# Spilling converted weights through GpSimd's DMA queue in place of SyncE's

## The chip, the core and the metric

The kernel runs on one core of a Trainium2 chip. The metric is the device time of one execution in microseconds (us). The core's engines work side by side, each through its own instructions in a fixed order: TensorE (PE; matmuls into PSUM), VectorE (DVE), ScalarE (ACT), GpSimd (POOL) and SyncE (SP). An engine waits at an instruction until what it needs is there, and everything behind it on that engine waits too. SyncE, GpSimd and ScalarE can ask for DMA transfers between the chip's large memory (DRAM) and its working memory (SBUF); each has its own queue of requests, and the transfers themselves run on 16 shared DMA engines.

## The reference

```python
def reference(q, k, v, cap, w1, w2, w3, w4, g):          # names shortened
    s = cap * tanh((q @ k.T) / sqrt(64) / cap)           # 4 batches, 12 heads, 448 x 448
    x = softmax(s) @ v                                   # -> 1792 tokens x 768
    h = x @ w1                                           # 768 -> 2048
    y = (h - tanh(h)) @ w2                               # 2048 -> 768
    h = y @ w3                                           # 768 -> 1024
    e = h * softmax(h)
    return ((e - mean(e)) / sqrt(var(e) + 1e-6) * g) @ w4   # 1024 -> 768
```

The weights come as 64-bit floats. The result is needed in 32 bits.

## The kernel before

**Halves and stages.** The four batches are done in two halves of two batches (`hb` 0 and 1), 896 tokens each. Each half runs through `attention`, `moe1` (w1, the tanh term and w2) and `moe2` (w3, softmax, norm and w4). Matmuls are done as three products of high and low parts (fp32r), so a weight is kept as a tile `w` of [128, 2, 512], high part first.

**Conversion and spill.** In the first half each weight unit is loaded as raw 64-bit words into a tile `st` (three buffers; line 106). VectorE puts a 32-bit float together in a tile `f` with three instructions (lines 111, 112, 113), ScalarE writes the high part into `w` (line 119, or 125 for w4), and VectorE the low part (line 120, or 126). There are 72 units. Each converted tile of 512 KB is then written to DRAM once by `keep` (line 136, "spill"): in order, five units behind the conversion (`DD` is 5), and the rest at the end of a stage. In the second half a unit is only read back from there (line 191, or 153 during attention). The tiles `w` take turns in 13 buffers, with one more (`wx`) in `moe1`; a buffer is free again when TensorE has used it and its spill has landed.

**Units of the first stage.** During attention the first 13 units are loaded by GpSimd's queue (in one case SyncE's) and converted beside it. Their spills stand at the end of that stage, in the `while pending: keep()` loop.

**moe1.** `up` (lines 459, 461) computes a block of 36 matmuls into a PSUM tile `hp`; `nonlinear` then has ScalarE (lines 487, 489, 491, 495, 501) and VectorE (493, 497, 496, 498, 502) turn it into `gh` and `gl`. Line 496, `t = h - t`, is the last to read `hp`. After the first four, the blocks share two PSUM buffers, so a block can begin when line 496 of the block two before it is done. `down` (lines 515, 517) multiplies by w2, and VectorE adds the result to `acc` (line 524). The weights for what follows are converted between these instructions.

**moe2.** `norm` ends in one GpSimd instruction, `rstd` to the power -0.5 (line 560); VectorE computes its input (line 559) and uses its output (line 561) ahead of TensorE's transposes (line 564).

**Order.** Attention is written out in order. In the other stages a scheduler orders the instructions of each engine ahead of time by its own estimate of durations and of what waits for what. So a change on one queue can move instructions on all engines.

```python
            pending.append((key, w))
            if len(pending) > DD:
                keep()
```

Of the kernel before, what the change touches and what calls it, by code (L numbers as in the profile page):

```python
# [9 lines left out]
F32 = mybir.dt.float32  # L10
# [19 lines left out]
def fused_kernel(ctx, tc, qk_in, v, cap, w1, w2, w3, w4, gln, out):  # L30
    nc = tc.nc
# [101 lines left out]
    def keep():  # L133
        key, w = pending.pop(0)
        d = drw.tile([P, 2, 512], F32R, name=f"d{key}")
        nc.sync.dma_start(d.bitcast(F32), w.bitcast(F32))
        saved[key] = d

    ahead = {}
# [38 lines left out]
    def unit(key, src, n, scale=None):  # L178

        pool, n2 = place["pool"]  # L180
        i = place["at"] = (place["at"] + 1) % (WA + n2)
        if key in ahead:
            w = ahead.pop(key)
            return w[:, 0], w[:, 1]
        if i < WA:
            w = wp.tile([P, 2, 512], F32R, tag="w", name="w")
        else:
            w = pool.tile([P, 2, 512], F32R, tag="wx", name="wx", bufs=n2)
        hi, lo = w[:, 0], w[:, 1]
        if key in saved:  # L190
            nc.sync.dma_start(w.bitcast(F32), saved[key].bitcast(F32))
        else:
            convert(hi, lo, src, n, scale)
# [3 lines that stand above are left out]
        return hi, lo  # L197
# [31 lines left out]
    def attention(ap, hb, xh, xl, rest=None):  # L229
# [214 lines left out]
        while pending:  # L444
            keep()
# [90 lines left out]
    def moe2(mp, hb, yh, yl):  # L536
# [113 lines left out]
        while pending:  # L650
            keep()
# [105 lines left out]
```

## Time and profile before

| what | us |
|---|---|
| median of 3 runs | 907.37 |
| lowest and highest run | 906.84, 908.77 |
| the profiled execution, its own time | 907.26 |
| its span in the trace | 905.5 |
| TensorE busy | 897.6 |
| VectorE busy | 613.4 |
| ScalarE busy | 416.7 |
| GpSimd busy | 48.1 |

The span runs from the first to the last instruction; the 1.76 us beside it are start and end of the execution. Busy is the time in which an engine has an instruction of its own in work; asking for transfers doesn't count. All times in the trace are us from the span's start. The first half of the work ends around 450 us. Matmuls overlap, so TensorE shows as busy even where it could go a little faster.

### The profile page before, as it was taken

The page shows a single profiled execution, that of the slowest core. Times are in us where ns is not written, and L with a number is a line of the kernel's source. Part 1 is how long each engine was busy: PE and PEld are TensorE (multiplying, and loading weights), DVE is VectorE, ACT ScalarE, POOL GpSimd, SP SyncE. Part 2 cuts the span into 40 slices and gives each one's busy share as a digit, 9 for nine tenths or more (in the row PEclk, how much of TensorE's full clock was granted, in tenths as well). Part 3 has the DMA queues.
Part 4 walks back from the last instruction along what each step waited for, and adds up shares of the span by engine and source line. Part 5 has one row for each costly group of instructions (what it writes and reads, how often), then busy time and mean ns, then how long its engine had stood idle before and what let it go on. Part 6 is the DMA issues. An engine that isn't in the chain of part 4 may idle for free.

```text
span 905.5 us, 12979 instructions
## 1 busy us (share of the span) xinstructions
PE 897.6 (99%) x5162; PEld 727.9 (80%) x5162; DVE 613.4 (68%) x954; ACT 416.7 (46%) x469; POOL 48.1 (5%) x88
## 2 busy tenths in 40 slices
PE   8999999999999999999999999999999999999998
PEld 5444699999989998888865448999999999888887
DVE  6687989899999990988257985970543634306841
ACT  7999276446254231443279871852512502113311
POOL 2211000000000000001022200000000000000000
PEclk9999999999999999999999999999999999999999
DMA  8554680796875873730256623433242432231301
GB/s 292 183 181 149 229 324 24 237 343 210 268 267 177 320 244 126 255 134 36 102 184 198 209 92 116 134 107 113 73 140 71 138 99 87 70 131 33 128 35 53
DMA packets 46424, 142.98 MB, mean 158 GB/s; under 512 B 10460, under 2 KB 13532, under 8 KB 46364
## 3 DMA queue, kind: packets, MB, share of 16 engines
q1 hardware_dynamic: 39180, 112.95, 36.6%
q0 software_dynamic: 7040, 29.20, 9.4%
q8 instruction: 41, 0.67, 0.3%
q14 instruction: 19, 0.16, 0.1%
q10 hardware_dynamic: 144, 0.00, 0.0%
HBM read 98.64 MB, written 43.33 MB: 157 GB/s over the span
## 4 chain that ended last, share of the span: by engine, by line
PE 84%; DVE 10%; DMA 3%; issue 1%; ACT 1%; SPq 0%; DVEq 0%
PE op L515 14%; PE hp L459 14%; PE op L517 7%; PE hp L461 7%; PE o L307 7%; PE hp L226 4%; PE hp L227 4%; PE hp L225 4%; PE s L275 4%; PE oab L615 2%; PE oab L619 2%; PE oab L616 2%; PE so L324 2%; DMA st<-in_moe_w_out_dram 2%; PE x L281 2%; PE tp L564 1%
## 5 line engine op out<-in xcount | busy, mean ns | idle before, releaser
L459 PE MATMUL hp<-xh,w 128*128 128x448 f32 x384 | 115.8, 368 | 1.5 <-DVE t L496 1.5
L459 PE MATMUL hp<-xl,w 128*128 128x448 f32 x384 | 115.8, 367 | 0.0
L461 PE MATMUL hp<-xh,w 128*128 128x448 f32 x384 | 115.7, 367 | 0.0
L517 PE MATMUL op<-gh,w 128*128 128x448 f32 x336 | 96.4, 367 | 0.0
L515 PE MATMUL op<-gl,w 128*128 128x448 f32 x336 | 96.1, 367 | 0.0
L515 PE MATMUL op<-gh,w 128*128 128x448 f32 x336 | 96.1, 367 | 0.0
L459 PEld LDWEIGHTS hp<-xh,w 128*128 128x128 f32 x384 | 71.8, 188 | 10.5 <-issue 2.5
L461 PEld LDWEIGHTS hp<-xh,w 128*128 128x128 f32 x384 | 72.1, 188 | 7.4 <-issue 0.7
L459 PEld LDWEIGHTS hp<-xl,w 128*128 128x128 f32 x384 | 72.1, 188 | 7.4 <-issue 0.7
L307 PE MATMUL o<-t,vf 128*32 128x448 f32 x768 | 77.8, 542 | 0.0
L299 ACT ACTIVATE t<-t,shift,capt 128x3136 f32<-128x3136 f32 (+2 forms) x26 | 72.8, 2807 | 0.7
L524 DVE TENSOR_TENSOR acc<-op,acc 128x448 f32<-128x448 f32 x72 | 41.9, 619 | 45.7 <-PE op L517 45.7
L515 PEld LDWEIGHTS op<-gl,w 128*128 128x128 f32 x336 | 63.1, 188 | 5.9
L515 PEld LDWEIGHTS op<-gh,w 128*128 128x128 f32 x336 | 63.0, 188 | 5.9
L517 PEld LDWEIGHTS op<-gh,w 128*128 128x128 f32 x336 | 63.1, 188 | 5.8
L292 ACT ACTIVATE t<-s,tscale 128x1344 f32<-128x1344 f32 x48 | 63.5, 1379 | 5.7 <-PE s L275 5.7
L225 PE MATMUL hp<-w,xh 128*128 128x512 f32 x168 | 65.5, 390 | 0.0
L227 PE MATMUL hp<-w,xl 128*128 128x512 f32 x168 | 65.4, 389 | 0.0
L226 PE MATMUL hp<-w,xh 128*128 128x512 f32 x168 | 65.4, 389 | 0.0
L501 ACT CAST gh<-gf 128x896 fp32r<-128x896 f32 x32 | 30.1, 944 | 73.8 <-PE op L517 47.8
L493 DVE SCALAR_TENSOR_TENSOR gf<-u,hp 128x896 f32<-128x896 f32 x32 | 34.8, 1088 | 41.2 <-ACT t L489 41.2
L487 ACT ACTIVATE u<-hp 128x896 f32<-128x896 f32 x32 | 29.5, 922 | 68.3 <-PE hp L461 68.3
(161 smaller groups left out, 1670.6 us busy)
## 6 DMA issues: line engine op xcount, KB each, us to landing
d<-w SPq DMA_DIRECT2D x69, 512.0 KB
w<-d SPq DMA_DIRECT2D x56, 512.0 KB
st<-in_moe_w_out_dram SPq DMA_DIRECT2D x35, 512.0 KB
st<-in_moe_w_in_dram SPq DMA_DIRECT2D x25, 512.0 KB
kq<-in_qk_dram POOLq DMA_DIRECT2D x21, 480.0 KB, 4.0
w<-d POOLq DMA_DIRECT2D x13, 512.0 KB, 5.2
st<-in_moe_w_in_dram POOLq DMA_DIRECT2D x11, 512.0 KB, 5.1
vf<-in_v_dram POOLq DMA_DIRECT2D x22, 256.0 KB, 3.2
```

Of the source, the lines that this page charges most:

```text
L225: nc.tensor.matmul(ps, sh, mh, start=first, stop=False)
L226: nc.tensor.matmul(ps, sh, ml, start=False, stop=False)
L227: nc.tensor.matmul(ps, sl_, mh, start=False, stop=last)
L275: nc.tensor.matmul(s[b // 3][:, b % 3, :S], st[rows, cs], mv[rows, KW:], start=first, stop=last)
L292: nc.scalar.activation(t[:, 3 * half:3 * half + 3], s[half][:, :, :S], AF.Tanh, scale=tscale)
L299: nc.scalar.activation(t[:, sl], t[:, sl], AF.Exp, bias=shift, scale=capt)
L307: nc.tensor.matmul(o[cs, :S], vf[:, r, cs], t[:, 6 if r == 3 else 2 * r + g // 2], start=(r == 0), stop=(r == 3))
L459: nc.tensor.matmul(hp[:, g, :S], wh[:, ms], xs[g][i], start=(kk == 0 and i == 0), stop=False)
L461: nc.tensor.matmul(hp[:, g, :S], wl[:, ms], xs[g][0], start=False, stop=(kk == NK - 1))
L515: nc.tensor.matmul(op[:, g, :S], wh, gg[i][:, g], start=(m == 0 and i == 0), stop=False)
L517: nc.tensor.matmul(op[:, g, :S], wl, gg[0][:, g], start=False, stop=(m == nm - 1))
L524: nc.vector.tensor_tensor(a, op[:, g, :S], a, ALU.add)
```

## The change

`keep` asks for the spill through GpSimd's queue and no longer through SyncE's. The data, the sizes and the number of transfers stay the same.

```diff
     def keep():
         key, w = pending.pop(0)
         d = drw.tile([P, 2, 512], F32R, name=f"d{key}")
-        nc.sync.dma_start(d.bitcast(F32), w.bitcast(F32))
+        nc.gpsimd.dma_start(d.bitcast(F32), w.bitcast(F32))
         saved[key] = d
```

The order of instructions changes on all engines of the first half. Three places follow.

VectorE, end of attention and the first block of `moe1`: `f<-st` are the three conversion instructions, line 493 the first instruction on a finished block. Before:

```order
L112 SCALAR_TENSOR_TENSOR f<-st,f 128x512
L113 SCALAR_TENSOR_TENSOR f<-st,f 128x512
L493 SCALAR_TENSOR_TENSOR gf<-u,hp 128x896
L497 SCALAR_TENSOR_TENSOR gf<-w,gf 128x896
L496 TENSOR_TENSOR t<-hp,t 128x896
```

And now:

```order
L112 SCALAR_TENSOR_TENSOR f<-st,f 128x512
L113 SCALAR_TENSOR_TENSOR f<-st,f 128x512
L111 TENSOR_SCALAR f<-st 128x512
L112 SCALAR_TENSOR_TENSOR f<-st,f 128x512
L493 SCALAR_TENSOR_TENSOR gf<-u,hp 128x896
L113 SCALAR_TENSOR_TENSOR f<-st,f 128x512
L497 SCALAR_TENSOR_TENSOR gf<-w,gf 128x896
L496 TENSOR_TENSOR t<-hp,t 128x896
```

One more unit is converted here, two of its instructions ahead of line 493 and one behind it.

VectorE in the third group of `up` blocks, between the ninth and the tenth line 496 of the program (`w<-f,w` is the low part of a converted unit). Before:

```order
L496 TENSOR_TENSOR t<-hp,t 128x896
L120 TENSOR_TENSOR w<-f,w 128x512
L498 COPY_PREDICATED gf<-mk,t 128x896
L111 TENSOR_SCALAR f<-st 128x512 x2
L112 SCALAR_TENSOR_TENSOR f<-st,f 128x512
L502 TENSOR_TENSOR gl<-gf,gh 128x896
L113 SCALAR_TENSOR_TENSOR f<-st,f 128x512
L493 SCALAR_TENSOR_TENSOR gf<-u,hp 128x896
L112 SCALAR_TENSOR_TENSOR f<-st,f 128x512
L496 TENSOR_TENSOR t<-hp,t 128x896
```

And now:

```order
L496 TENSOR_TENSOR t<-hp,t 128x896
L497 SCALAR_TENSOR_TENSOR gf<-w,gf 128x896
L120 TENSOR_TENSOR w<-f,w 128x512
L498 COPY_PREDICATED gf<-mk,t 128x896
L120 TENSOR_TENSOR w<-f,w 128x512
L111 TENSOR_SCALAR f<-st 128x512 x2
L112 SCALAR_TENSOR_TENSOR f<-st,f 128x512
L502 TENSOR_TENSOR gl<-gf,gh 128x896
L493 SCALAR_TENSOR_TENSOR gf<-u,hp 128x896
L113 SCALAR_TENSOR_TENSOR f<-st,f 128x512
L496 TENSOR_TENSOR t<-hp,t 128x896
```

Line 497 now stands behind the first of the two, a second line 120 has come in, and one line 112 has moved ahead.

GpSimd around the norms of the first half (the `d` tiles are spills, `kq` and `vf` loads for the second half's attention). Before, its row of seven `rstd` follows the loads:

```order
L243 DMA kq<-in_qk_dram 128x960 x3
L249 DMA vf<-in_v_dram 128x512
L560 TENSOR_TENSOR rstd<-rstd,mhalf 128x1 x7
L243 DMA kq<-in_qk_dram 128x960
```

And now:

```order
L136 DMA d_3_3790<-w 128x1024
L136 DMA d_4_3803<-w 128x1024
L560 TENSOR_TENSOR rstd<-rstd,mhalf 128x1 x2
L136 DMA d_5_3805<-w 128x1024
L136 DMA d_5_3807<-w 128x1024
L136 DMA d_6_3809<-w 128x1024
L136 DMA d_7_3811<-w 128x1024
L136 DMA d_7_3813<-w 128x1024
L560 TENSOR_TENSOR rstd<-rstd,mhalf 128x1 x5
```

All 72 spills stand in GpSimd's order now: 13 behind its last load of the first attention, 48 ahead of the four loads that stood ahead of `rstd`, six between those loads and the first `rstd`, and the last five between the second and the third.

## Rows read from the trace of the kernel before

**Rows 1.** Page, part 1: busy us (share of the span) xinstructions.

```profile
PE 897.6 (99%) x5162; PEld 727.9 (80%) x5162; DVE 613.4 (68%) x954; ACT 416.7 (46%) x469; POOL 48.1 (5%) x88
```

**Rows 2.** Windows: stretch, its us, busy us by engine, PEclk, DMA share, GB/s.

```profile
170.00:190.00 20.00, 20.00 (x99) 18.16 (x98) 17.11 (x29) 9.60 (x17) 0.00 (x0) 1.00 0.97 312
...
250.00:275.00 25.00, 23.46 (x115) 21.15 (x114) 23.28 (x35) 14.45 (x19) 0.00 (x0) 1.00 0.73 252
275.00:335.00 60.00, 60.00 (x298) 55.62 (x297) 58.91 (x101) 20.07 (x31) 0.00 (x0) 1.00 0.72 252
```

**Rows 3.** Timeline of TensorE at four block starts: start, us, [idle before <-releaser].

```profile
202.96 0.37 PE L459 MATMUL hp<-xh,w 128*128 128x448 f32 x1
...
210.26 0.57 PE L459 MATMUL hp<-xh,w 128*128 128x448 f32 x2
...
262.76 0.44 PE L459 MATMUL hp<-xh,w 128*128 128x448 f32 x1 [1.25 <-DVE t L496]
...
270.58 0.44 PE L459 MATMUL hp<-xh,w 128*128 128x448 f32 x1 [0.29 <-DVE t L496]
```

**Rows 4.** Timeline of VectorE, first L493 and the four gates.

```profile
122.24 1.09 DVE L493 SCALAR_TENSOR_TENSOR gf<-u,hp 128x896 f32<-128x896 f32 x1 [2.12 <-ACT t L489]
...
201.63 1.08 DVE L496 TENSOR_TENSOR t<-hp,t 128x896 f32<-128x896 f32 x1
...
208.85 1.09 DVE L496 TENSOR_TENSOR t<-hp,t 128x896 f32<-128x896 f32 x1
...
260.53 1.08 DVE L497 SCALAR_TENSOR_TENSOR gf<-w,gf 128x896 f32<-128x896 f32 x1
261.53 1.08 DVE L496 TENSOR_TENSOR t<-hp,t 128x896 f32<-128x896 f32 x1
...
269.35 1.08 DVE L496 TENSOR_TENSOR t<-hp,t 128x896 f32<-128x896 f32 x1
```

**Rows 5.** Waits of SyncE's queue: us in total, times, longest.

```profile
SPq L106 <- DVE f L113: 89.8, 42, 7.6
```

**Rows 6.** Timeline of SyncE's queue: spills after attention, one later load.

```profile
105.17 14.82 SPq L136 DMA_DIRECT2D d<-w  x13
...
179.06 0.33 SPq L106 DMA_DIRECT2D st<-in_moe_w_out_dram  x1
```

**Rows 7.** Timeline of VectorE in a run of conversions.

```profile
178.35 0.68 DVE L113 SCALAR_TENSOR_TENSOR f<-st,f 128x512 uint32<-128x512 uint32 x1
...
181.24 0.43 DVE L111 TENSOR_SCALAR f<-st 128x512 uint32<-128x512 uint32 x1 [1.61 <-DMA st<-in_moe_w_out_dram]
181.58 0.69 DVE L113 SCALAR_TENSOR_TENSOR f<-st,f 128x512 uint32<-128x512 uint32 x1
182.18 0.69 DVE L120 TENSOR_TENSOR w<-f,w 128x512 fp32r<-128x512 f32 x1
182.79 0.69 DVE L112 SCALAR_TENSOR_TENSOR f<-st,f 128x512 uint32<-128x512 uint32 x1
...
184.85 0.43 DVE L111 TENSOR_SCALAR f<-st 128x512 uint32<-128x512 uint32 x1 [0.18 <-DMA st<-in_moe_w_out_dram]
```

**Rows 8.** Waits of VectorE for loads, 119 to 275.

```profile
DVE f L111 <- DMA st<-in_moe_w_out_dram: 4.4, 4, 1.6
...
DVE f L111 <- DMA st<-in_moe_w_in_dram: 1.0, 1, 1.0
```

**Rows 9.** Timeline of GpSimd: last load of attention, third rstd.

```profile
79.88 0.54 POOL L106 DMA_DIRECT2D st<-in_moe_w_out_dram  x1 [2.00 <-DVE rs L361]
...
407.37 0.55 POOL L560 TENSOR_TENSOR rstd<-rstd,mhalf 128x1 f32<-128x1 f32 x1 [18.81 <-DVE rstd L559]
```

**Rows 10.** Page, part 6: issues by GpSimd, KB each, median us to landing.

```profile
w<-d POOLq DMA_DIRECT2D x13, 512.0 KB, 5.2
...
st<-in_moe_w_out_dram POOLq DMA_DIRECT2D x1, 512.0 KB, 3.8
```

**Rows 11.** Instructions on tile st: ns min/median/max, first and last start.

```profile
L111 DVE TENSOR_SCALAR f<-st x72: 402/421/482, 11.4 to 395.1; 128x512 uint32<-128x512 uint32 x72
```

## The prediction

> **What bounds the kernel now.** I read the page's busy shares first, then busy time by stage, then TensorE's own stalls, then what the two engines beside it wait for. TensorE is busy 897.6 us, 99% of the span [rows 1], at a granted clock of 1.00 in each stretch shown [rows 2], the higher of its two levels. So a change that adds no arithmetic can win only what TensorE stands still, and the stages say where that is. The 72 spills stand in the first half: conversion and both expert layers of the first two batches. There TensorE is busy in all of a stretch such as 170 to 190 or 275 to 335, and loses time in one place, 250 to 275, where it is busy 23.46 of 25 us [rows 2]. Its order of instructions shows two stalls in that stretch, 1.25 us before 262.76 and 0.29 us before 270.58 [rows 3], both ended by VectorE's L496. They are the whole gain on offer: 1.54 us.
>
> VectorE is the second bound. It is busy 17.11 of 20 us from 170 to 190, 23.28 of 25 from 250 to 275 and 58.91 of 60 from 275 to 335 [rows 2]. Its L496 is the last reader of a PSUM tile hp; two blocks of 36 matmuls later, TensorE needs that buffer. In the four places shown, L496 ends at 202.71, 209.94, 262.61 and 270.43 [rows 4] (start plus duration), and TensorE begins the block that takes the buffer at 202.96, 210.26, 262.76 and 270.58 [rows 3]. The margins are 0.25 and 0.32 us in the first pair and none in the second, where a start follows the end by 0.15 us. Call these gates 9, 10, 13 and 14, by the count of L496 in the program. Whatever makes VectorE later there by more than the margin makes TensorE later.
>
> **The change: what it takes off SyncE.** SyncE issues the weight loads (L106) and, between them, the spills (L136), each after a wait for its own data. The loads don't suffer from that. A load needs one of three st buffers, and L113 frees it: SyncE waited 42 times for that, 89.8 us in all [rows 5], so it was at the load before the buffer was there. One example: L113 ends at 179.03 [rows 7] and the load is issued at 179.06 [rows 6]. The only long block of spills ahead of loads, 13 of them in 14.82 us from 105.17 [rows 6], falls where VectorE next waits for ScalarE (the 2.12 us before 122.24 [rows 4]) and not for a load. So I put the freed issue time of SyncE at nothing; the cover is the wait for st, and without it a spill's 1.14 us (14.82 through 13) would be what a load gains.
>
> **What it adds to GpSimd.** GpSimd is idle in this half but for the seven rstd of each norm. An issue takes it 0.54 us [rows 9]. Six spills now stand ahead of the first two rstd and five ahead of the third. The third starts at 407.37, after GpSimd has waited 18.81 us for VectorE's L559 [rows 9]. Five issues, 2.7 us, fit into that wait, and the tiles that they spill are converted ahead of that L559 in VectorE's own order: hidden. If a tile were late, its lateness would pass straight to rstd and, through VectorE, to TensorE's transposes. The first 13 spills leave as soon as GpSimd's last load of the attention stage is issued (79.88 plus 0.54 [rows 9]), not at 105.17. I cost that at nothing too: at that time TensorE works from tiles already loaded, and the small transfers of the softmax sums are used two iterations later; without that distance they would share up to 14.8 us of transfers (13 times 1.14).
>
> **What it moves.** Here I expect the price. The scheduler, which no longer sees loads behind spills, hands VectorE conversions earlier (L111, L112, L113, then L120), and VectorE works in order. I counted the instructions ahead of each gate in both orders. More than before stand there: at gate 9, two L111, two L112, two L113 and one L120, less one L497 (it now follows its L496); at gate 10, two L111, one L112, two L113 and two L120; at gate 13, one L111, two L112, two L113 and one L120, less one L497; at gate 14, two of each of the first three and one L120, less one L497.
>
> From start to next start, L111 takes 0.34 us (181.24 to 181.58), L113 0.60, L120 0.61 [rows 7], L112, of L113's length, 0.60 as well, and L497 1.00 (260.53 to 261.53 [rows 4]). So:
> - gate 9: 0.68 + 1.20 + 1.20 + 0.61 - 1.00 = 2.69 us
> - gate 10: 0.68 + 0.60 + 1.20 + 1.22 = 3.70 us
> - gate 13: 0.34 + 1.20 + 1.20 + 0.61 - 1.00 = 2.35 us
> - gate 14: 0.68 + 1.20 + 1.20 + 0.61 - 1.00 = 2.69 us
>
> One L111 and one L112 of these, 0.94 us, stand ahead of the first L493 and fall into the 2.12 us that VectorE waited there anyway. That leaves 1.75, 2.76, 1.41 and 1.75 us.
>
> Now TensorE, step by step, each start 0.15 us behind its L496. Gate 9: 202.71 + 1.75 + 0.15 = 204.61, 1.65 us late. Gate 10: 209.94 + 2.76 + 0.15 = 212.85; TensorE, late already, would have come at 211.91, so 0.94 us more. Gate 13: without its stall it came at 261.51, now at 264.10; VectorE lets it go at 262.61 + 1.41 + 0.15 = 264.17. Gate 14: 270.43 + 1.75 + 0.15 = 272.33 against 270.58 before. What is lost at gates 9 and 10 thus replaces the old stalls at 13 and 14, and 1.75 us stay. From 275 on TensorE is never held up in the rows of before [rows 2], and nothing gives the time back.
>
> **The loads' landing** is the unknown. From 119 to 275 VectorE waits for a load five times, 5.4 us [rows 8]; the one issued at 179.06 [rows 6] is used at 184.85, 5.8 us later, after such a wait of 0.18 us. Now a spill on GpSimd's queue runs beside the load and not behind it, with the DMA engines at 0.97 from 170 to 190 [rows 2]. From below: a half-megabyte load that GpSimd asked for alone landed in 3.8 us; were all loads as quick, 2 us off each wait, all 5.4 us of waiting could go. From above: weight reloads on the same queue, between two other loads, take a median of 5.2 us, 1.4 us more than that one [rows 10]; five waits make 7 us. The bytes to move are the same and the engines are the limit in the bursts, so I stay near the middle and take a tenth of the upper bound: 0.7 us.
>
> Sum: 907.26 us (the profiled execution's own time, 0.11 under the median of 907.37) + 1.75 + 0.7 = 909.7 us. Less than 0.2%, 1.8 us, can't be told from no change here.
>
> **The rivals.**
> 1. *The extra work is absorbed; no change.* The conversions done early are missing later, and VectorE's waits for loads between the gates (5.4 us) could take in the 1.75 us. For it: conversion bursts are paced by loads. Against it: a load is issued when VectorE frees a buffer, so a later VectorE makes later loads. About 907.3 us.
> 2. *Faster.* Loads no longer share SyncE's queue with spills. If they land in about 4 us, VectorE gains most of the 5.4 us, which covers 1.75 us of extra work, and both old stalls go: 907.26 - 1.54 = 905.7 us. It decides from about 3.3 us of saved waits (1.75 + 1.54). Against it: the 0.97 in the burst.
> 3. *Much slower by the loads.* Half of the upper bound comes, 3.5 us: 907.26 + 1.75 + 3.5 = 912.5 us.
> 4. *GpSimd's issues hold VectorE up.* L111 takes 402 to 482 ns with a median of 421 [rows 11]; if every one of the 30 between 122 and 270 took the longest, VectorE loses 30 times 0.061 = 1.8 us on top: 911.5 us. The Trainium skill, "SBUF — State Buffer", section "Who interferes with whom", has VectorE in a two-port mode and GpSimd lock each other out for a whole instruction, and its section on the two sides warns of spills issued from GpSimd for that reason. In this trace the spread of L111 is no more than those 80 ns.
>
> **How the numbers follow.** My forecast (907.26 + 1.75 and up to 2 us on it) 0.36; absorbed 0.32; faster 0.14; much slower by loads 0.10; held up by GpSimd 0.08. The forecast's case reaches down to 909.0, so a little of it falls within 0.2%: slower 0.51, same 0.35, faster 0.14. The range takes in rival 1 whole, most of rival 2's way and rival 3: 906.2 to 912.6 us.
>
> **What would show it.** Right: TensorE waits for L496 at gates 9 and 10 (about 203 to 213), in sum some 2.6 us; loads still issued 0.03 us after L113; the step from L111 to L113 unchanged; the rstd of the first half not later against their L559. Wrong: no wait of TensorE before 250; VectorE's waits for loads from 119 to 275 well under 5.4 us (rival 2) or over 8 (rival 3); L111 with a median over 0.44 us (rival 4); a wait of VectorE for rstd, which would mean that spills do stand in its way.

## The result, and the profile after

The changed kernel is slower: 916.04 us against 905.01 in the same session (medians of 9 runs each). The ratio of the two kernels' runs is 1.0105, 95% interval 1.008 to 1.013; that of the medians alone would be 1.0122. The runs of the kernel before lie between 901.83 and 910.25 us, so a single time says little. The forecast was 2.4 us more than before; some 9.5 us came (0.0105 times 907). The profiled execution took 918.89 us, its span 917.1, 11.6 us more than before.

**Page part 1 and waits, changed kernel** (busy us; waits: us in total, times, longest):

```profile
PE 902.1 (98%) x5162; PEld 732.3 (80%) x5162; DVE 614.4 (67%) x954; ACT 416.7 (45%) x469; POOL 89.4 (10%) x160
```

```profile
PE hp L459 <- DVE t L496: 6.8, 4, 4.1
...
PE hp L459 <- DVE xh L387: 1.8, 2, 1.6
```

VectorE works as long as before [rows 1], but TensorE now waits 8.6 us for it, against 1.54. The starts of TensorE's stalled blocks tell where. In the first, the last xh tiles of attention are late; then hp is missing at gate 5, which the prediction didn't name, and at gates 9, 13 and 14 [rows 3].

```profile
113.25 0.47 PE L459 MATMUL hp<-xh,w 128*128 128x448 f32 x1 [1.58 <-DVE xh L387]
...
150.21 0.64 PE L459 MATMUL hp<-xh,w 128*128 128x448 f32 x2 [1.89 <-DVE t L496]
...
213.02 1.09 PE L459 MATMUL hp<-xh,w 128*128 128x448 f32 x2 [4.07 <-DVE t L496]
213.91 0.95 PE L459 MATMUL hp<-xl,w 128*128 128x448 f32 x2
214.66 0.95 PE L461 MATMUL hp<-xh,w 128*128 128x448 f32 x2
215.40 0.95 PE L459 MATMUL hp<-xh,w 128*128 128x448 f32 x2
216.15 0.62 PE L459 MATMUL hp<-xl,w 128*128 128x448 f32 x2
216.61 0.57 PE L461 MATMUL hp<-xh,w 128*128 128x448 f32 x2
217.03 0.57 PE L459 MATMUL hp<-xh,w 128*128 128x448 f32 x2
...
274.64 0.65 PE L459 MATMUL hp<-xh,w 128*128 128x448 f32 x2 [0.41 <-DVE t L496]
...
282.77 0.44 PE L459 MATMUL hp<-xh,w 128*128 128x448 f32 x1 [0.46 <-DVE t L496]
```

Behind the stall of 4.07 us a pair of matmuls takes 0.75 us, soon 0.41 again: eight matmuls take 3.13 us and not 1.65, which is 1.5 us more. Behind the stall of 1.89 us it is 1.3 us more. The windows show it as the granted clock (us, busy us by engine, PEclk, DMA share, GB/s):

```profile
150.00:170.00 20.00, 19.80 (x90) 18.26 (x91) 18.37 (x23) 11.41 (x14) 1.06 (x2) 0.91 0.18 60
170.00:190.00 20.00, 20.00 (x101) 18.53 (x100) 17.52 (x30) 7.96 (x17) 3.91 (x7) 1.00 0.84 306
210.00:230.00 20.00, 16.98 (x75) 15.41 (x76) 20.00 (x26) 10.92 (x14) 1.59 (x3) 0.91 0.54 188
250.00:275.00 25.00, 24.59 (x120) 22.04 (x119) 22.33 (x37) 10.14 (x14) 2.66 (x5) 1.00 0.81 281
275.00:335.00 60.00, 59.54 (x294) 54.75 (x293) 58.05 (x92) 23.11 (x33) 7.70 (x13) 1.00 0.66 227
```

The stalls are 7.1 us more than before (8.6 less 1.5); with 2.8 us at the lower clock that makes 9.9 of the 11.6 us. Another 0.8 us stands ahead of the first spill: GpSimd's last load of attention is issued at 80.66 and not at 79.88 [rows 9]. Now VectorE's timeline:

```profile
99.47 0.23 DVE L361 SCALAR_TENSOR_TENSOR rs<-rs,gcol 56x16 f32<-56x16 f32 x1 [4.12 <-DMA rs<-su]
...
126.86 0.43 DVE L111 TENSOR_SCALAR f<-st 128x512 uint32<-128x512 uint32 x1 [2.01 <-DMA st<-in_moe_w_out_dram]
...
211.79 1.08 DVE L496 TENSOR_TENSOR t<-hp,t 128x896 f32<-128x896 f32 x1
...
219.92 1.08 DVE L496 TENSOR_TENSOR t<-hp,t 128x896 f32<-128x896 f32 x1
...
273.41 1.08 DVE L496 TENSOR_TENSOR t<-hp,t 128x896 f32<-128x896 f32 x1
...
281.56 1.07 DVE L496 TENSOR_TENSOR t<-hp,t 128x896 f32<-128x896 f32 x1
```

VectorE waits 4.12 us for a small transfer in attention and 2.01 us for a load ahead of the first L493. Gate 1 comes 6.1 us later than before, and gates 9, 10, 13 and 14 come 10.2, 11.1, 11.9 and 12.2 us later than in [rows 4]. Its waits for loads from 119 to 275 are 11.7 us, against 5.4 [rows 8]:

```profile
DVE f L111 <- DMA st<-in_moe_w_out_dram: 8.8, 7, 2.1
DVE f L111 <- DMA st<-in_moe_w_in_dram: 2.9, 2, 2.7
```

In the queues' timelines, the first spills leave right behind GpSimd's last load, at 81.19, as forecast. SyncE then takes more than twice as long to ask for the small transfers (2.4 us for two of rs, against 1.17 before). First GpSimd, then SyncE:

```profile
81.19 0.62 POOL L136 DMA_DIRECT2D d<-w  x1
81.96 3.14 POOL L136 DMA_DIRECT2D d<-w  x6 [0.15 <-issue]
...
88.35 2.42 SPq L357 DMA_DIRECT2D rs<-su  x2
90.90 1.28 SPq L364 DMA_DIRECT2D rd<-rs  x1
92.29 2.97 SPq L370 DMA_DIRECT2D rb<-rd  x2
```

L111 and the third rstd [rows 9, 11] are as they were, the latter 12.3 us later like all else there:

```profile
L111 DVE TENSOR_SCALAR f<-st x72: 407/423/484, 11.7 to 407.4; 128x512 uint32<-128x512 uint32 x72
```

```profile
419.64 0.56 POOL L560 TENSOR_TENSOR rstd<-rstd,mhalf 128x1 f32<-128x1 f32 x1 [6.00 <-DVE rstd L559]
```

### The profile page after: what moved, and what is told of

It reads as the page before. It is cut to its first block, busy times and chain, and to the rows that moved or that the text cites. A ratio compares the mean times of both kernels' runs of the same rounds, so it can differ in the third digit from the quotient of the medians.

```text
span 917.1 us, 13030 instructions
## 1 busy us (share of the span) xinstructions
PE 902.1 (98%) x5162; PEld 732.3 (80%) x5162; DVE 614.4 (67%) x954; ACT 416.7 (45%) x469; POOL 89.4 (10%) x160
## 4 chain that ended last, share of the span: by engine, by line
PE 82%; DVE 8%; DMA 4%; issue 3%; ACT 2%; SPq 0%; DVEq 0%
PE op L515 15%; PE hp L459 14%; PE op L517 8%; PE hp L461 7%; PE o L307 5%; PE hp L226 4%; PE hp L227 4%; PE hp L225 4%; PE s L275 4%; PE oab L615 2%; PE oab L619 2%; PE oab L616 2%; PE x L281 2%; PE so L324 1%; DMA st<-in_moe_w_out_dram 1%
## 5 line engine op out<-in xcount | busy, mean ns | idle before, releaser
L459 PE MATMUL hp<-xh,w 128*128 128x448 f32 x384 | 117.7, 373 | 8.7 <-DVE t L496 6.8
L459 PE MATMUL hp<-xl,w 128*128 128x448 f32 x384 | 116.7, 370 | 0.0
L461 PE MATMUL hp<-xh,w 128*128 128x448 f32 x384 | 116.6, 370 | 0.0
L517 PE MATMUL op<-gh,w 128*128 128x448 f32 x336 | 96.3, 367 | 0.0
L515 PE MATMUL op<-gh,w 128*128 128x448 f32 x336 | 96.3, 367 | 0.0
L515 PE MATMUL op<-gl,w 128*128 128x448 f32 x336 | 96.1, 367 | 0.0
L459 PEld LDWEIGHTS hp<-xh,w 128*128 128x128 f32 x384 | 72.4, 190 | 19.2 <-issue 7.9
L459 PEld LDWEIGHTS hp<-xl,w 128*128 128x128 f32 x384 | 73.1, 190 | 7.4 <-issue 0.7
L517 PEld LDWEIGHTS op<-gh,w 128*128 128x128 f32 x336 | 63.1, 188 | 5.9
L515 PEld LDWEIGHTS op<-gl,w 128*128 128x128 f32 x336 | 63.1, 188 | 5.8
L515 PEld LDWEIGHTS op<-gh,w 128*128 128x128 f32 x336 | 63.1, 188 | 5.8
L119 ACT CAST w<-f 128x512 fp32r<-128x512 f32 x44 | 27.3, 622 | 86.6 <-DVE f L113 66.8
L136 POOL DMA_DIRECT2D d<-w x69 | 39.6, 575 | 270.7 <-DVE w L120 195.5
L493 DVE SCALAR_TENSOR_TENSOR gf<-u,hp 128x896 f32<-128x896 f32 x32 | 34.7, 1085 | 39.5 <-ACT t L489 39.5
```

The lines of the kernel that those rows point to most:

```text
L136: nc.gpsimd.dma_start(d.bitcast(F32), w.bitcast(F32))
L459: nc.tensor.matmul(hp[:, g, :S], wh[:, ms], xs[g][i], start=(kk == 0 and i == 0), stop=False)
L461: nc.tensor.matmul(hp[:, g, :S], wl[:, ms], xs[g][0], start=False, stop=(kk == NK - 1))
L515: nc.tensor.matmul(op[:, g, :S], wh, gg[i][:, g], start=(m == 0 and i == 0), stop=False)
L517: nc.tensor.matmul(op[:, g, :S], wl, gg[0][:, g], start=False, stop=(m == nm - 1))
```

## The experiments

The change has three parts that can be taken apart: the 13 spills of attention's end, the 59 later ones, and the order that the scheduler made. All ratios are to the kernel before, of the same chip and session, with 95% intervals. "Gate 9" is the end of the ninth L496 in the profiled execution; "waits" are VectorE's for loads between the ends of gates 8 and 9 (us). S is SyncE's queue, G is GpSimd's. An order of its own is the one that the scheduler made for that kernel.

| kernel | 13 / 59 spills | order | ratio | gate 9 | waits |
|---|---|---|---|---|---|
| before | S / S | before | 1 | 202.71 | 2.8 |
| changed | G / G | its own | 1.0105 (1.008 to 1.013) | 212.87 | 5.7 |
| att_on_sync | S / G | its own | 1.0120 (1.0086 to 1.0154) | 211.47 | 10.6 |
| att_on_gpsimd | G / S | its own | 1.0034 (1.0010 to 1.0057) | 204.83 | 1.8 |
| att_held_back | G, later / G | changed | 1.0111 (1.0077 to 1.0145) | 210.23 | 5.8 |
| att_early_sync | S, early / S | its own | 1.0044 (1.0013 to 1.0075) | 209.01 | 1.8 |
| att_held_rest_sync | G, later / S | att_on_gpsimd | 1.0024 (1.0001 to 1.0047) | 206.26 | 1.6 |
| order_before | G / G | before | 1.0044 (1.0022 to 1.0066) | 209.39 | 5.0 |
| order_before_att_sync | S / G | before | 1.0038 (1.0014 to 1.0061) | 204.39 | 4.4 |
| order_after_on_sync | S / S | changed | 1.0075 (1.0048 to 1.0102) | 210.40 | 2.7 |
| order_att_all_sync | S / S | att_on_sync | 1.0097 (1.0069 to 1.0126) | 210.62 | 8.8 |
| order_att_l113_first | S / S | the same, L113 moved | 1.0072 (1.0045 to 1.0098) | 208.61 | 6.1 |
| before_l113_first | S / S | before, L113 moved | 1.0003 (0.9979 to 1.0026) | 203.48 | 2.3 |
| two_spills_back | S / G, two S | before | one run: 904.74 us | 203.58 | 3.3 |
| one_queue_gpsimd | S / G, loads G | before | 1.0059 (1.0035 to 1.0083) | 204.69 | 3.7 |
| loads_on_gpsimd | S / S, loads G | before | 1.0073 (1.0045 to 1.0100) | 207.58 | 6.8 |

### Which spills: att_on_sync, att_on_gpsimd, att_held_back, att_early_sync

```diff
-    def keep():
+    def keep(eng=nc.gpsimd):          # att_on_gpsimd, att_early_sync: nc.sync
...
         while pending:
-            keep()
+            keep(nc.sync)             # att_on_gpsimd: nc.gpsimd
```

att_held_back puts `nc.gpsimd.tensor_copy(hold, rbs[n - 2][:, :1])` behind `finish2(n - 2)`; att_early_sync calls `keep` from the third last iteration of attention on.

> The 13 spills at the end of attention go back to SyncE's queue; the other 59 stay on GpSimd's. Theory A (crowding: the 13 spills, let go at 81 us, delay the small transfers of the softmax sums, VectorE ends attention 5 us late and never makes it up): the wait of 4.1 us for rs is gone, the 13 spills leave near 105 us, and the time is that of the kernel before within 0.3%, 902 to 908 us beside 905. Theory B (the prediction's: the rest of the change gives VectorE more to do ahead of its L496 at the gates): 1 to 3 us above the kernel before, with waits of TensorE for L496 of 3 us or more before 250 us. If both hold, in between.

> Only the 13 spills at the end of attention go to GpSimd's queue; the other 59 stay on SyncE's. Theory A (crowding by these 13): most of the loss is here, 1.0% over the kernel before, some 914 us; VectorE waits about 4 us for rs near 95 us, and its first L496 comes about 6 us later than before. Theory B (the other 59 make the loss through VectorE's order): within 0.3% of the kernel before, whatever VectorE waits near 95 us.

> All 72 spills on GpSimd's queue as in the changed kernel, but GpSimd first copies one column of the last rb tile, so that the first 13 spills leave at about 106 us and not at 81. Theory A (it is the early start of the 13 that costs): no wait for rs over 1 us, and 905 to 909 us, at least 7 us less than the changed kernel. Theory C (it is the second queue in itself that slows the transfers, at any time): 912 us or more. Theory B: 907 to 911 us, with waits of TensorE for L496 before 250 us.

> All spills on SyncE's queue as in the kernel before, but the first nine of the 13 stand there right behind the rs transfers issued at about 80 us, two more follow one by one. Theory A (crowding, on whichever queue): slower than the kernel before by 5 us or more, with VectorE waiting for rs or rb between 85 and 105 us, since here the small transfers also stand behind the spills in one queue. Theory C (only a second queue beside SyncE's does harm): within 0.3% of the kernel before.

Theory A fell. With the 13 spills back on SyncE, or held back, all of the loss stays (1.0120, 1.0111). The second is the cleaner pair: att_held_back came out with the changed kernel's order, instruction for instruction, and only the 13 leave later. No rs is late there, but the L111 that this order puts ahead of the first L493 waits 4.49 us, gate 1 is still 4.9 us late, and later waits follow. With the 13 alone on GpSimd 0.34% is lost, though VectorE waits 4.25 us for rs there and gate 1 is 5.5 us late. Early on SyncE they do like harm (1.0044, and VectorE waits 5.02 us for rs), so rs can be late without a second queue; how much of the 0.44% is that wait isn't shown, since this kernel's order differs too. Theory B's 1 to 3 us for att_on_sync is too little, and theory C's 912 us or more for att_held_back came (median 915.97).

Among these kernels and the changed one, the waits between gates 8 and 9 are 1.8 us where the 59 stay on SyncE, and 5.7 or more where they are on GpSimd. In att_on_sync VectorE's first eight gates agree with the kernel before to 0.03 us, and from 174 on the order differs. Timeline of VectorE, att_on_sync:

```profile
174.03 0.69 DVE L112 SCALAR_TENSOR_TENSOR f<-st,f 128x512 uint32<-128x512 uint32 x1
176.18 0.43 DVE L111 TENSOR_SCALAR f<-st 128x512 uint32<-128x512 uint32 x1 [1.46 <-DMA st<-in_moe_w_in_dram]
176.52 0.68 DVE L113 SCALAR_TENSOR_TENSOR f<-st,f 128x512 uint32<-128x512 uint32 x1
```

The kernel before at that place:

```profile
174.05 0.69 DVE L112 SCALAR_TENSOR_TENSOR f<-st,f 128x512 uint32<-128x512 uint32 x1
174.77 0.69 DVE L113 SCALAR_TENSOR_TENSOR f<-st,f 128x512 uint32<-128x512 uint32 x1
176.46 0.43 DVE L111 TENSOR_SCALAR f<-st 128x512 uint32<-128x512 uint32 x1 [1.00 <-DMA st<-in_moe_w_in_dram]
```

L113, which frees the buffer st, now stands behind an L111 that waits for another load. The load that needs the buffer is asked for at 177.23 and not at 175.49. Theory D says that such places in the order make the loss.

### The order without the queue, the queue without the order

Here an ordering edge between each instruction and the next on its engine fixes the order of another kernel on TensorE, VectorE and ScalarE (an edge orders the issue and waits for nothing). Inside attention, where the order is written by hand, none is added. The loads keep their order in all of these kernels; where SyncE's spills stand between its loads isn't fixed and changes with the order.

```diff
         fused_kernel(tc, *args)
+        put_in_order(nc, tc)          # the order of the kernel named in the table
...
+    for before, here in zip(names, names[1:]):
+        tc.add_manual_dep(traced[here], before, mybir.DependencyInfo(
+            mybir.DependencyClass.NoSync, mybir.DependencyReason.DATA), reason="order")
```

> All 72 spills on GpSimd's queue, as in the changed kernel, but TensorE, VectorE and ScalarE have the kernel before's order of instructions, word for word. Theory D (the order costs: L113, which frees the buffer for a load, stands behind another L111 that waits for a load, so waits add up ahead of gate 9): only what the early 13 spills cost is left, 905 to 909 us as with these 13 alone on GpSimd (908.6). Theory C (the second queue makes loads land later at any time): 913 us or more, as the changed kernel (916).

> The order of the kernel before on TensorE, VectorE and ScalarE, the 13 spills of attention's end on SyncE's queue, the other 59 on GpSimd's. Against the kernel with the same queues and its own order (916.7) only the order differs. Theory D: the time of the kernel before within 0.3%, 902 to 907.5 us, waits of VectorE for loads from 119 to 275 us between 4 and 8 us, and gate 9 within 1 us of 202.71. Theory C: 913 us or more, with gate 9 several us late.

> All 72 spills on SyncE's queue as in the kernel before, but the changed kernel's order of instructions on TensorE, VectorE and ScalarE. Theory D: 911 us or more although no queue is changed, with waits of TensorE for L496 at gates 9 and 10 of 3 us or more in sum, and VectorE waiting 9 us or more for loads from 119 to 275. Theory C: within 0.4% of the kernel before.

> Only the 13 spills of attention's end on GpSimd's queue, held back until the last rb tile has landed (about 106 us); the other 59 on SyncE's queue. SyncE then asks for the three loads at about 117 to 120 us some 3 to 4 us earlier than in the kernel before. If the early start of the 13 is what costs 0.3% in the kernel with these 13 alone on GpSimd, this one is at 903 to 906 us, no slower than the kernel before, with no wait for rs; if it is the scheduler's order, the loss of 0.3% or more stays.

Both theories hold in part. All spills on GpSimd in the old order cost 0.44%, so 0.6% of the changed kernel's 1.05% go with the order (0.3 to 0.9% by the two intervals); the changed order costs 0.75% with every spill on SyncE. ScalarE's order and the places of SyncE's spills change along with VectorE's, and they weren't tried apart. With every spill on SyncE the price is paid at another place than theory D named: TensorE waits 1.45 us at gates 9 and 10, not 3, but the L111 that now stands ahead of the first L493 waits 6.27 us. Its load stands behind the 13 spills on SyncE; timelines of SyncE and VectorE (L191 and L196 are L106 and L111 here):

```profile
120.07 1.22 SPq L191 DMA_DIRECT2D st<-in_moe_w_out_dram  x1
```

```profile
127.48 0.43 DVE L196 TENSOR_SCALAR f<-st 128x512 uint32<-128x512 uint32 x1 [6.27 <-DMA st<-in_moe_w_out_dram]
```

The place in the queue explains little of that. In att_held_rest_sync, where the same L111 stands ahead of the first L493, the 13 are on GpSimd and the load is asked for 3.6 us earlier, yet the L111 waits 5.72 us:

```profile
116.50 0.34 SPq L106 DMA_DIRECT2D st<-in_moe_w_out_dram  x1
```

```profile
125.91 0.43 DVE L111 TENSOR_SCALAR f<-st 128x512 uint32<-128x512 uint32 x1 [5.72 <-DMA st<-in_moe_w_out_dram]
```

In both the DMA engines are full around it, with a share of 1.02 from 116 to 120 and over 1.00 from 120 to 124, which points to the spills' transfers on whichever queue. Between gates 8 and 9 the changed order costs nothing with one queue (waits of 2.7 us), and 3 us more waiting with two (5.7). The 13 spills on GpSimd instead of SyncE are 0.06% in the old order (order_before against order_before_att_sync), below what the intervals can tell, though TensorE has stalls of 2.5 us at 109 to 115 in the first and none there in the second. Held back on GpSimd, with the rest on SyncE, they cost 0.24%, which can't be told from the 0.34% of att_on_gpsimd.

What the second queue does is seen in order_before_att_sync: up to gate 8 it is the kernel before to within 0.25 us, then one load is late. GpSimd's and VectorE's timelines:

```profile
173.27 0.53 POOL L222 DMA_DIRECT2D d<-w  x1 [2.00 <-DVE w L206]
174.21 0.53 POOL L222 DMA_DIRECT2D d<-w  x1 [0.41 <-DVE w L206]
```

```profile
178.51 0.43 DVE L197 TENSOR_SCALAR f<-st 128x512 uint32<-128x512 uint32 x1 [0.73 <-DMA st<-in_moe_w_out_dram]
178.85 0.68 DVE L199 SCALAR_TENSOR_TENSOR f<-st,f 128x512 uint32<-128x512 uint32 x1
179.45 0.69 DVE L198 SCALAR_TENSOR_TENSOR f<-st,f 128x512 uint32<-128x512 uint32 x1
182.95 0.43 DVE L197 TENSOR_SCALAR f<-st 128x512 uint32<-128x512 uint32 x1 [2.81 <-DMA st<-in_moe_w_out_dram]
```

(L197 to L199, L206 and L222 are L111 to L113, L120 and L136 here.) The load asked for at 175.27 is used 7.7 us later, against 5.75 before, and gate 9 is 1.7 us late. The DMA share is 0.95 from 172 to 183. On SyncE the first of the two spills stood behind that load and the second behind the next; on GpSimd they leave when their data is there. The Trainium skill, "DMA: Bandwidth & Descriptors", section "Issuing engines are not separate DMA queues", says that transfers started by ScalarE, SyncE or GpSimd run on the same 16 DMA engines and interleave. The trace agrees: SyncE's load takes 7.7 us and not 5.75 with GpSimd's two spills beside it.

### Is it these spills, and is it the split?

```diff
         key, w = pending.pop(0)
+        if key in ("1_2_0_2", "1_2_1_0"):      # two_spills_back
+            eng = nc.sync
...
-        ff = narrowed(words(src))
+        ff = narrowed(words(src, nc.gpsimd))   # one_queue_gpsimd, loads_on_gpsimd
```

In one_queue_gpsimd the loads and the 59 spills also keep, on GpSimd, the order among each other that SyncE had; in two_spills_back SyncE's loads keep theirs.

> As order_before_att_sync, but the two spills that GpSimd asked for at 173.27 and 174.21, just ahead of the load asked for at 175.27 that landed 1.9 us later than before, go back to SyncE, each behind the load that it followed in the kernel before. Theory E: that load lands in 6.0 us or less (7.7 there, 5.75 before), VectorE waits under 2 us for it, and gate 9 is within 0.6 us of 202.71. The rival, that the many spills together do it: gate 9 still 1.2 us late or more. One look; the time itself can't tell 1.7 us.

> The order of the kernel before on TensorE, VectorE and ScalarE; the loads of the weights (L106) go to GpSimd's queue too, with the 59 later spills between them in the very order that SyncE had; the 13 spills of attention's end on SyncE. So loads and spills share one queue again, another one. Theory E (a queue is served in order, so a spill behind a load isn't asked for before that load; with a second queue it leaves once its data is there and takes transfer time from the load that VectorE waits for): gate 9 within 0.6 us of 202.71, VectorE's waits for loads between gates 8 and 9 under 3.5 us, and the time of the kernel before within 0.3%. Theory F (GpSimd's queue is slower in itself): gate 9 1.5 us late or more, and 0.4% or more slower.

> The order of the kernel before on TensorE, VectorE and ScalarE; all spills on SyncE's queue, the loads of the weights (L106) on GpSimd's. Two queues again, with the roles exchanged. Theory E: spills no longer stand behind loads, so 0.2 to 0.6% slower, gate 9 1 to 3 us late. Theory F (GpSimd's queue is the slow one): all loads land later, 0.8% or more slower and gate 9 more than 3 us late. If the split doesn't matter: within 0.2%.

Two spills account for most of what is lost there: the load, asked for at 175.66, now lands within 5.3 us, and VectorE (L201 is L111) waits 1.04 us for it.

```profile
180.94 0.43 DVE L201 TENSOR_SCALAR f<-st 128x512 uint32<-128x512 uint32 x1 [1.04 <-DMA st<-in_moe_w_out_dram]
```

The stretch from gate 8 to 9 takes 39.2 us, against 40.3 with them on GpSimd and 38.5 before. Gate 9 is 0.9 us late, a little more than expected, since VectorE now waits 0.99 us for a later load. One run can't show what this is worth in time. Theory E fell as to a single queue: on GpSimd alone, in SyncE's order, it is no better (1.0059, and gate 9 is 2.0 us late), as theory F had it. GpSimd asks for a load later once it is free to. Timelines of one_queue_gpsimd (L204 is L113, L197 the load):

```profile
176.03 0.69 DVE L204 SCALAR_TENSOR_TENSOR f<-st,f 128x512 uint32<-128x512 uint32 x1
```

```profile
177.02 0.53 POOL L197 DMA_DIRECT2D st<-in_moe_w_out_dram  x1 [2.78 <-DVE f L204]
```

L113 ends at 176.72, the request follows 0.30 us later, where SyncE took 0.03 [rows 6, 7]. In loads_on_gpsimd the split and the later requests come together, and it is slower still in the trace: gate 9 is 4.9 us late, as F had it (more than 3). Its 0.73% lies between E's 0.2 to 0.6% and F's 0.8% or more, and with its interval can't tell them apart.

### Which part of the order

```diff
-L111 TENSOR_SCALAR f<-st 128x512
 L113 SCALAR_TENSOR_TENSOR f<-st,f 128x512
+L111 TENSOR_SCALAR f<-st 128x512
```

This was done at 14 places of att_on_sync's order (order_att_l113_first) and at 13 of the order before (before_l113_first); order_att_all_sync has att_on_sync's order as it is.

> All spills on SyncE's queue; TensorE, VectorE and ScalarE have the order of the kernel att_on_sync, in which VectorE waited 10.56 us for loads between gates 8 and 9 and gate 9 was 8.8 us late. If that order costs by itself (L113 behind a waiting L111): the waits stay at 8 us or more, gate 9 is 7 us late or more, and 0.9% or more slower. If it takes the second queue to make it cost: waits of 3 to 6 us, gate 9 under 4 us late, and 0 to 0.5% slower.

> As order_att_all_sync (all spills on SyncE, 0.97% slower, gate 9 7.9 us late, VectorE's waits for loads between gates 8 and 9 8.8 us), but with L113 of a unit, at the 14 places where it stood behind the L111 of a later unit, put right ahead of that L111. The instructions ahead of each gate stay the same; only the buffer st is given back before VectorE waits for the next load. If the position of L113 makes the waits: they fall to 5 us or less, gate 9 is 2 to 5 us late (the 2.5 us of additional instructions stay), and 0.2 to 0.6% slower. If the additional instructions or ScalarE's order are what costs: gate 9 still 7 us late, and 0.8% or more slower.

> The kernel before with that one edit: at 13 places L113 right ahead of the L111 of a later unit behind which it stood; TensorE's and ScalarE's order and the queues as before. If the position of L113 makes waits: VectorE's waits for loads from 119 to 275 fall from 5.4 to under 4 us, the stalls of 1.25 and 0.29 us at gates 13 and 14 shrink or vanish, and the time is 0 to 0.2% under that of the kernel before. If not: the same waits, stalls and time.

The order of att_on_sync costs 0.97% with every spill on SyncE: it needs no second queue. Of its 8.8 us of waits, 2.7 go with L113's place; gate 9 comes from 7.9 to 5.9 us late, gate 13 from 10.8 to 6.6. The intervals of the two ratios overlap, so this gain is seen in one trace each and not in the times. The 5.9 us that stay are more than the additional instructions, two L111 and three L112 or L113 between gates 8 and 9: 0.68 + 1.80 = 2.5 us. The rest are waits for loads (6.1 us, against 2.8 before). A conversion drawn ahead of a gate needs its load earlier, and loads come no faster: with three buffers SyncE asked for one every 3.0 us here before (eight intervals from 172.62 to 196.37), and every 3.3 us in order_att_all_sync (eight from 173.59 to 200.03).

In the kernel before, the move changes nothing that can be measured (1.0003). The waits from 119 to 275 fall from 5.4 to 3.8 us, the stall at gate 13 falls to 0.50 us, that at gate 14 stays at 0.29, and a new one of 0.45 us comes at gate 9. No version was shown to beat the kernel before.

## Why the prediction was wrong

Its direction was right, its size too small by some 7 us. Point by point:

- **What bounds it**: right. Apart from the clock, TensorE lost only where VectorE came late, and the first half never gave the time back. The places are half right: gates 9, 13 and 14 as named, no wait at gate 10, and two that weren't named, xh at the end of attention (1.58 us) and gate 5 (1.89).
- **SyncE's freed issue time at nothing**: right for the old order. Loads still follow L113 by 0.03 us, and where a load was asked for 3.6 us earlier VectorE still waited 5.72 us for it, against 6.27 (att_held_rest_sync, order_after_on_sync).
- **GpSimd's rstd hidden**: right; the five spills ahead of the third are issued by 413.6, and it still waited 6 us for L559.
- **The 13 spills "at nothing too"**: wrong in the trace. The prediction named the cover, small transfers used two iterations later, and what it would cost without it. The cover was too short: VectorE waited 4.12 us for rs. What that is worth in time stays open: the pairs above give 0.06% and 0.34%, with intervals that overlap, and with the 13 held back in the same order the loss is as large (1.0111).
- **The moved instructions, 1.75 us**: the step that failed. It priced a conversion ahead of a gate by its instructions alone. The runs show that the changed order costs 0.6 to 0.75% (5.5 to 7 us). By the traces that is the loads: the conversions' own loads are awaited, and L113 behind a waiting L111 delays the next load. Whether ScalarE's order has a share wasn't tried. The 0.94 us ahead of the first L493, which were to fall into a wait, brought a wait for their own load of 2.01 us, and of 6.27 with the spills ahead of it.
- **The loads' landing, 0.7 us**: mis-sized. The 59 spills on the second queue, in the old order, cost 0.38% (0.14 to 0.61), some 3.4 us; the one load late by 1.9 us is where it begins.
- **The lower clock** behind stalls, 2.8 us, was no term of the sum; the prediction gives no reason for leaving it out.
- **The rivals**: 3 had the nearest time, 912.5, and its sign came true, load waits of 11.7 us (over 8), but for the order more than for the landing: these waits are 12.6 us with the changed order on SyncE alone, and 6.4 with every spill on GpSimd in the old order. 4 is out: L111's median is 423 ns against 421. Of the lockout that the Trainium skill, "SBUF — State Buffer", section "Who interferes with whom", states for both engines, VectorE's side doesn't show in L111's times; GpSimd's may, in nine requests of 0.76 us or more beside an L111 (last section). 1 and 2 are out.

## What to carry to other kernels

An instruction that a scheduler moves ahead of a critical one costs what it waits for, and not only its duration; price it by the pace of the loads behind it. Ask of each new order what frees a load's buffer, and whether that now stands behind another wait. A write on a second queue no longer stands behind the reads of the first, and where the DMA engines are full it takes its time from them. A burst of writes that is moved out of one wait's way can land in another's: here the 13 spills cost VectorE 4 us at rs when they left early, and 4 to 6 us at a load when they left late under the changed order.

## What the hardware showed that was not expected

- **The clock behind a stall.** After stalls of 1.89 and 4.07 us TensorE ran at the lower of its two levels for some 3 us (granted 0.91 on the mean of 20 us). The length of a stall alone doesn't decide it: att_held_back stalled for up to 3.1 us with 1.00 in every window.
- **Two paces at a granted clock of 1.00.** In the kernel before, 19 pairs of matmuls take 7.85 us at one place and 20 pairs 8.11 at another: 206.6 and 202.8 ns for a matmul. Which one holds changes within an execution, and from one to the next. The traces show what it weighs: from the first L459 of the second half to its last L515 or L517, a stretch that no edit touches and in which TensorE stalls for under 0.3 us, six of the sixteen traces take 238.5 to 238.7 us and ten take 242.2 to 243.0. So the pace alone can part two runs by some 4 us. The 904.74 us of two_spills_back, whose trace is of the shorter kind where the kernel before's is of the longer, show no gain. What sets the pace isn't shown. TensorE's timeline, before (rows of pairs):

```profile
175.27 0.57 PE L517 MATMUL op<-gh,w 128*128 128x448 f32 x2
...
183.12 0.57 PE L515 MATMUL op<-gh,w 128*128 128x448 f32 x2
...
229.73 0.56 PE L515 MATMUL op<-gh,w 128*128 128x448 f32 x2
...
237.84 0.56 PE L517 MATMUL op<-gh,w 128*128 128x448 f32 x2
```

- **Slow requests.** While seven spills of GpSimd were under way, SyncE took 2.42 us for two small requests that take 1.17 otherwise, and 1.28 for one that takes 0.36 to 0.40. It doesn't take a second queue: in att_early_sync SyncE took 1.56 us for that one, right behind nine spills of its own. The DMA share was 1.0 in both.
- **GpSimd's request beside a conversion.** In the changed kernel nine of the 72 spills took GpSimd 0.76 to 1.16 us to ask for, not 0.53, and in each of the nine an L111 of VectorE begins 0.21 to 0.29 us after the request does. 14 others overlap an L111 at another place and take 0.53 to 0.55 us. VectorE's L111 isn't longer. GpSimd's and VectorE's timelines, changed kernel:

```profile
182.81 0.76 POOL L136 DMA_DIRECT2D d<-w  x1 [2.75 <-DVE w L120]
```

```profile
183.03 0.42 DVE L111 TENSOR_SCALAR f<-st 128x512 uint32<-128x512 uint32 x1
```
